# A decode step bound by its loads: 32 small GpSimd loads added beside the K pairs

## The chip, the core and the metric

The kernel runs on one core of a Trainium2 chip. The core has a matrix engine (TensorE, in the profile PE, its weight loads PEld), VectorE (DVE), ScalarE (ACT), GpSimd (POOL) and SyncE (SP), which share one on-chip memory of 128 partitions, and sixteen DMA engines that move data between it and the chip's main memory. SyncE issues the loads; the other engines can issue some too. The metric is the device time of one execution in microseconds (us): the median of the runs.

## The reference

One step of decoding for four sequences mixes two branches with a gate.

```python
x = A_x                                              # [4, 1, 1024]
g = sigmoid((x * gate_w).sum(-1, keepdims=True))
# A: attention of one query per head over a cache, 32 heads of 128, 8192 keys
q = (x @ wq).reshape(4, 1, 32, 128).transpose(0, 2, 1, 3)
p = softmax(einsum("bhqd,bhkd->bhqk", q, k_cache) * 128 ** -0.5)
a = einsum("bhqk,bhkd->bhqd", p, v_cache).transpose(0, 2, 1, 3).reshape(4, 1, 4096) @ wo
# B: with one token per sequence, the token that is selected is always that token
r = x @ w_r
b = x + ((silu(x @ w_gate) * (x @ w_up)) @ w_down) * sigmoid(r)
return g * a + (1 - g) * b
```

All is bfloat16. The two caches are 4 x 32 x 8192 x 128 values each, 268 MB; the weights wq, wo (8.4 MB each) and w_gate, w_up, w_down (7.3 MB each) come on top: some 576 MB are read once, and little is computed with each value.

## The kernel before

Everything large goes through one ring, the tile `ring`: eleven units of 16 KB per partition (2 MB each). A K or V pair is the cache of four heads of one sequence, 8.4 MB in four units, with 64 KB in each partition. There are 32 K pairs and 32 V pairs. A list written out by hand (`plan`) says at which place of the ring each load goes, and `load_pair` (L194) issues it on SyncE, mostly as one DMA (L204), sometimes as two (L209). A load that overwrites a place waits until TensorE has read what was there; SyncE's queue is in order. The order of all work is given by hand (the schedule of TensorE, VectorE and GpSimd is manual): first wq, the three small loads of x, w_r and gate_w into the tile `x` (L228 to L230), and w_gate; then K pairs 0 to 7 (with w_up behind pair 1); then K pair d and V pair d - 8 in turns; then w_down and the last V pairs; at the end wo in pieces of shrinking size.

For a K pair (`k_pair`, L494) there are eight steps. In each, VectorE transposes an eighth of the pair in place (L511, blocks of 32 x 32 words) and TensorE multiplies it, eight matmuls of 512 columns, with the query of the pair laid out in the tile `Z` (L516), summing into `S_ps`. There are two Z tiles, used in turns. GpSimd fills the Z of pair d + 1 with four small copies (`spread`, L492), which stand in its stream at step 4 of pair d. They wait until the matmuls of pair d - 1, the last that read the same Z, have ended. Eight K pairs make a group, behind which softmax runs (VectorE, ScalarE), and GpSimd and ScalarE copy the probabilities into the tile `PB` (L568, L570). V pairs multiply them with V (L587), 64 matmuls each.

The tile `x` (`x6`, L227) has the four rows of x, the row w_r and the row gate_w in partitions 0 to 5, 2 KB in each. TensorE transposes it once at the start (L254), and near the end `add_x` reads its four rows of x again. GpSimd issues no DMA: its stream holds memsets, copies and the waits for them.

Of the kernel before, what the change touches and what calls it, by code (L numbers as in the profile page):

```python
# [8 lines left out]
BF = mybir.dt.bfloat16  # L9
# [103 lines left out]
def kernel(  # L113
# [15 lines left out]
    nc = tc.nc  # L129
    P = 128  # L130
    Bn, Sq, D = A_x.shape
    _, H, Sk, Dh = A_k_cache.shape
    F = B_w_gate.shape[1]
    DT = D // P
# [27 lines left out]
    const = ctx.enter_context(tc.tile_pool(name="const", bufs=1))  # L162
# [31 lines left out]
    def load_pair(src, n, cuts=(1, 1), second=None):  # L194

        place, down = next(plan)
        lo = place * UN
        if second is None:
            second = place * UN + n if place + 4 <= NU else 0
        at = [lo, second]  # L200
        assert second or (n == RING and lo + n == NU * UN and not down)
        halves = [flat[:, x:x + n] for x in at]
        if cuts == (1, 1) and second == lo + n:
            nc.sync.dma_start(out=flat[:, lo:lo + 2 * n], in_=src)  # L204
        else:
            for i, half in enumerate(halves):
                step = n // cuts[i]
                for x in range(0, n, step):
                    nc.sync.dma_start(out=half[:, x:x + step], in_=src[:, i * n + x:i * n + x + step])  # L209
        return halves, list(range(RD))[::-1] if down else list(range(RD))  # L210
# [5 lines left out]
    def bank(ps, z, shape, dtype=F32):  # L216
        b = ps[:, z] if dtype == F32 else ps[:, z].bitcast(dtype)
        n = 1
        for k in shape:
            n *= k  # L220
        names = "abcd"[:len(shape)]
        return b[:, 0:n].rearrange("p (%s) -> p %s" % (" ".join(names), " ".join(names)), **dict(zip(names, shape)))
# [1 line left out]
    N = H * Dh  # L224
    wq_at, _ = load_pair(A_wq.rearrange("(c t) n -> c (t n)", t=DT), DT // 2 * N)
    NX = Bn + 2
    x6 = const.tile([NX, D], BF)  # L227
    nc.sync.dma_start(out=x6[0:Bn], in_=x2)  # L228
    nc.sync.dma_start(out=x6[Bn:Bn + 1], in_=B_w_r.rearrange("(o n) -> o n", o=1))
    nc.sync.dma_start(out=x6[Bn + 1:Bn + 2], in_=gate_w.rearrange("(o n) -> o n", o=1))  # L230
# [8 lines left out]
    n = 1  # L239
# [10 lines left out]
    identb = const.tile([P, P], BF)  # L250
    nc.gpsimd.tensor_copy(out=identb[:], in_=ident[:])
    xw_ps = bank(S0, 2, [DT, NX], BF)
    for t in range(DT):
        nc.tensor.transpose(out=xw_ps[:, t, :], in_=x6[:, t:D:DT], identity=identb[0:NX, 0:NX])  # L254
    xw = const.tile([P, DT, NX], BF)
    nc.vector.tensor_copy(out=xw[:], in_=xw_ps)  # L256
    xT = [xw[:, t, 0:Bn] for t in range(DT)]
# [1 line left out]
    for half in range(2):  # L259
        for e in range(2):  # L260
            nc.gpsimd.tensor_copy(out=R[:, 2 * half + e].rearrange("p (n j) -> p n j", n=4),
                                  in_=ident[:, 64 * half + e:64 * half + 64:2].unsqueeze(1).to_broadcast([P, 4, 32]))
# [205 lines left out]
    def flush():  # L468
        while pending:
            pending.pop(0)()  # L470

    def flush_sums():
        while full:
            full.pop(0)()

    def flush_late():
        while late:
            late.pop(0)()
# [4 lines left out]
    def kv_view(cache, d):  # L483
        b, h0 = heads(d)
        return cache[b, h0:h0 + NQ].rearrange("h (r j) d -> (h r) (j d)", j=2 * JR)

    def spread(d):
        b, h0 = heads(d)
        Z = Zt[d % 2]
        for q in range(NQ):  # L490
            at = slice(QP * q, QP * (q + 1))
            nc.gpsimd.tensor_copy(out=Z[at, :, QP - 1 + QP * q], in_=qa[at, :, h0 + q, b])  # L492

    def k_pair(d):  # L494
        g, t = divmod(d, GD)
        Z = Zt[d % 2]
        if d == 0:
            spread(0)
        if t == 0:
            S_ps[g] = S0  # L500
        sps = S_ps[g]
        ks, order = load_pair(kv_view(A_k_cache, d), RING)
        flush_sums()
        for k, n in enumerate(order):
            unit = ks[n // JT][:, (n % JT) * UN:(n % JT + 1) * UN]
            kn = unit.bitcast(U32).rearrange("p (j h i) -> p h j i", j=CJ, h=2)
            T = unit.rearrange("p (j h i e) -> p h j i e", j=CJ, h=2, e=2)
            s = QP - 1 - (RD * t + n)
            for half in range(2):
                step = 2 * k + half  # L510
                nc.vector.transpose(out=kn[:, half], in_=kn[:, half])  # L511
                if step < 2 and ahead:
                    ahead.pop(0)()
                for e in range(2):
                    for z in range(4):
                        nc.tensor.matmul(sps[:, z, :], lhsT=Z[:, 2 * half + e, s:s + P], rhs=T[:, half, 16 * z:16 * z + 16, :, e],  # L516
                                         start=(t + k + half + e == 0),
                                         stop=(t == GD - 1 and k == RD - 1 and half + e == 2))
                if step == RD and d + 1 < ND:
                    spread(d + 1)  # L520
                if step == RD:
                    flush()
                if step == RD + 2:
                    flush_late()
        if t == GD - 1:
            ahead.extend(softmax(g))
            while g > 0 and ahead:
                ahead.pop(0)()

    def softmax(g):  # L530
        sps = S_ps.pop(g)
        PTs = turned(P, 4 * NB)

        def first():

            nc.vector.tensor_reduce(out=mx[:, 0:1], in_=sps[:].rearrange("p z n -> p (z n)"), axis=AX.X, op=ALU.max)  # L536
            nc.vector.transpose(out=mxT[:].bitcast(U32), in_=mx[:].bitcast(U32))
            gm = stat.tile([P, GD], F32, tag="gm")
            nc.vector.tensor_reduce(out=gm[:], in_=mxT[:].rearrange("p (t r) -> p t r", r=RD), axis=AX.X, op=ALU.max)
            nc.vector.tensor_scalar(out=ng[:].rearrange("p (t r) -> p t r", r=RD), in0=gm[:].unsqueeze(2).to_broadcast([P, GD, RD]),  # L540
                                    scalar1=-scale, scalar2=None, op0=ALU.mult)
            nc.vector.transpose(out=ngT[:].bitcast(U32), in_=ng[:].bitcast(U32))  # L542
            negm = ngT
            rs = stat.tile([P, 1], F32, tag="rs")
            nc.scalar.activation(out=PTs, in_=sps[:].rearrange("p z n -> p (z n)"), func=ACT.Exp, bias=negm[:, 0:1], scale=scale, accum_out=rs[:, 0:1])  # L545
            rs_t[g] = rs

        def second():
            PT = ptp.tile([P, CJ, 32], BF, name="PT", tag="PT")
            nc.vector.transpose(out=PT[:].rearrange("p j i -> p (j i)"), in_=PTs)  # L550
            PT_t[g] = PT
            if g == 0:
                spread_p(0, NW)
            elif g == NG - 1:
                spread_p(GD * g, NW - 1)

        return [first, second]
# [103 lines left out]
    for kind, d in order:  # L661
        if kind == "k":
            k_pair(d)
            if d in side:
                side[d]()
            if d == ND - 1:
                scores.close()
                fin = ctx.enter_context(tc.tile_pool(name="fin", bufs=1, space=PSUM))
                A_ps.extend(fin.tile([P, NB], F32, name=f"acc{n}") for n in range(NH))
                A_ps.append(fin.tile([P, 2, NB], F32, name="led"))  # L670
                wd_piece()
                add_x()
        if (kind, d) == ("v", ND - 1):
            first, second = wo_two(0)
            first()
            last = [second]
        if kind == "v":
            v_pair(d)
        if (kind, d) == ("v", ND - 2):
            o_rows(0, GE)  # L680
# [47 lines left out]
```

## Time and profile before

| What | Value |
|---|---|
| median of 3 runs | 1340.88 us (1340.85 to 1340.89) |
| profiled execution | 1340.96 us, its span 1339.2 us |
| TensorE matmuls, busy | 1031.3 us (77%) |
| VectorE, busy | 638.7 us (48%) |
| GpSimd, busy | 67.0 us (5%) in 174 instructions |
| moved by DMA | 576.14 MB, mean 430 GB/s |
| a K load, issue to landing (median) | 27.5 us |
| packets under 512 bytes | 1436 of 13032 |

The span is the time from the first instruction to the last in the profiled execution; the rest of its time lies around it. A line of waits reads: engine, what it works on and its line, who let it go, then the sum of those waits, how many there were, and the longest. A line of the timeline reads: start and length in us, engine, line, operation, what it writes and reads with shapes, how many instructions are merged, and in brackets the idle time before it and what ended that. In the chain of work that ended last, DMA has 67%, TensorE 22%, VectorE 9%. A queue's line has its packets, its MB and the time of its packets as a share of sixteen engines' span.

### The profile page before, as it was taken

To read this page: it belongs to the slowest core of one execution; us is meant where nothing else is said; L and a number is where in the kernel's file an instruction comes from. 1 tells how busy PE (TensorE), PEld (TensorE's weight loads), DVE (VectorE), ACT (ScalarE), POOL (GpSimd) and SP (SyncE) were. 2 spreads that over 40 slices of the span, in tenths; PEclk is the share of its full clock that TensorE was granted. 3 is DMA by queue.
4 is the path that set the end of the run, shared out by engine and by line. 5 is a ranking of instruction groups with operands and counts; after the bars stand their busy time and mean duration, and the time that the engine had idled before them with its cause. 6 is when DMAs were issued, how large, how long until landed. Compare 5 with 4: busy or idle time off the path is not lost.

```text
span 1339.2 us, 6936 instructions
## 1 busy us (share of the span) xinstructions
PE 1031.3 (77%) x4654; PEld 139.8 (10%) x1486; DVE 638.7 (48%) x385; ACT 57.7 (4%) x58; POOL 67.0 (5%) x174
## 2 busy tenths in 40 slices
PE   2386787887777788777787977777797778687887
PEld 0011000001010010101001110100111011111111
DVE  2285998556553436555352556634345556100001
ACT  0000000100010000100010000100000000110000
POOL 2000000100010000100010000100001000100000
PEclk9697998898888998888889988888998889689999
DMA  9999999999999999999999999999999999999998
GB/s 415 433 437 437 435 437 435 420 438 433 433 435 437 427 433 435 429 438 431 433 431 433 435 439 427 429 433 435 438 430 428 433 429 429 438 429 445 422 422 352
DMA packets 13032, 576.14 MB, mean 430 GB/s; under 512 B 1436, under 2 KB 1700, under 8 KB 1970
## 3 DMA queue, kind: packets, MB, share of 16 engines
q1 hardware_dynamic: 12994, 575.69, 99.6%
q8 instruction: 24, 0.39, 0.1%
q14 instruction: 6, 0.05, 0.0%
q10 hardware_dynamic: 8, 0.00, 0.0%
HBM read 575.68 MB, written 0.01 MB: 430 GB/s over the span
## 4 chain that ended last, share of the span: by engine, by line
DMA 67%; PE 22%; DVE 9%; POOL 0%; ACT 0%; issue 0%; SPq 0%
DMA ring<-in_A_k_cache_dram 53%; PE S_ps L516 15%; DMA ring<-in_A_v_cache_dram 10%; DVE ring L511 9%; PE o_ps L587 5%; DMA ring<-in_B_w_gate_dram 3%; DMA ring<-in_A_wo_dram 2%; PE o_ps L342 1%; POOL PB L570 0%; DVE mx L536 0%; PE led L633 0%; ACT TB L545 0%; PE acc L296 0%; POOL Z L492 0%; PE o_ps L633 0%
## 5 line engine op out<-in xcount | busy, mean ns | idle before, releaser
L511 DVE STREAM_TRANSPOSE ring<-ring 128x2048 uint32<-128x2048 uint32 x256 | 566.5, 2276 | 307.7 <-DMA ring<-in_A_k_cache_dram 307.7
L516 PE MATMUL S_ps<-ring,Z 128*128 128x512 bf16 x2048 | 519.9, 408 | 229.3 <-DVE ring L511 216.1
L587 PE MATMUL o_ps<-ring,PB 128*64 128x512 bf16 x2048 | 457.4, 384 | 35.7 <-DMA ring<-in_A_v_cache_dram 33.3
L516 PEld LDWEIGHTS <-Z 128*128 128x128 bf16 x512 | 53.0, 104 | 683.0 <-issue 683.0
L617 DVE SCALAR_TENSOR_TENSOR OS<-o_ps,mE,OS 128x512 f32<-128x512 f32 x33 | 24.8, 751 | 161.7 <-ACT OS L613 160.2
L587 PEld LDWEIGHTS <-PB 128*64 128x64 bf16 x512 | 56.7, 111 | 428.3 <-issue 427.6
L625 DVE SCALAR_TENSOR_TENSOR OS<-o_ps,mE,OS 128x512 f32<-128x512 f32 x5 | 3.7, 750 | 143.6 <-ACT OS L623 143.6
L492 POOL COPY Z<-qa 32x4 bf16<-32x4 bf16 x128 | 25.8, 201 | 716.7 <-PE S_ps L516 689.6
L570 POOL COPY PB<-PT 32x1024 bf16<-32x1024 bf16 (+3 forms) x23 | 33.4, 1452 | 466.6 <-PE o_ps L587 360.7
L613 ACT ACTIVATE OS<-o_ps,mE 128x512 f32<-128x512 f32 x11 | 7.6, 687 | 671.2 <-PE o_ps L587 671.2
L568 ACT COPY PB<-PT 32x1024 bf16<-32x1024 bf16 (+3 forms) x21 | 30.3, 1444 | 22.4 <-PE o_ps L587 17.4
L545 ACT ACTIVATE TB<-S_ps,mx 128x2048 bf16<-128x2048 f32 x4 | 7.9, 1967 | 321.7 <-DVE mx L542 321.7
L254 PE MATMUL S_ps<-identb,x 6*128 6x6 bf16 x8 | 0.6, 196 | 22.3 <-DMA x<-in_gate_w_dram 22.3
L342 PE MATMUL o_ps<-ring,xw 128*4 128x512 bf16 (+2 forms) x128 | 12.9, 490 | 3.5 <-DMA ring<-in_B_w_gate_dram 3.5
L633 PEld LDWEIGHTS o_ps<-selg,OS 128*128 128x128 f32 x88 | 11.5, 191 | 8.8 <-issue 8.5
L550 DVE STREAM_TRANSPOSE PT<-TB 128x2048 bf16<-128x2048 bf16 x4 | 9.2, 2312 | 6.4 <-ACT TB L545 6.4
L296 PE MATMUL acc<-ring,hT 128*4 128x512 bf16 x54 | 7.9, 466 | 5.5 <-DMA ring<-in_B_w_down_dram 5.5
L536 DVE TENSOR_REDUCE mx<-S_ps 128x1 f32<-128x2048 f32 x4 | 9.1, 2282 | 6.0 <-PE S_ps L516 6.0
L296 PE MATMUL acc<-ring,LT 128*4 128x512 bf16 x64 | 8.8, 378 | 3.3 <-DMA ring<-in_A_wo_dram 2.8
L633 PE MATMUL o_ps<-selg,OS 128*128 128x8 f32 x88 | 10.5, 245 | 0.0
L623 ACT ACTIVATE OS<-o_ps,mE 128x512 f32<-128x512 f32 x5 | 3.4, 687 | 151.2 <-PE o_ps L587 151.2
L256 DVE COPY xw<-S_ps 128x48 bf16<-128x48 bf16 x1 | 0.2, 184 | 17.5 <-PE S_ps L254 17.5
(83 smaller groups left out, 88.4 us busy)
## 6 DMA issues: line engine op xcount, KB each, us to landing
ring<-in_A_v_cache_dram SPq DMA_DIRECT2D x7, 4096.0 KB
ring<-in_A_k_cache_dram SPq DMA_DIRECT2D x6, 4096.0 KB, 33.9
ring<-in_A_v_cache_dram SPq DMA_DIRECT2D x6, 2048.0 KB, 28.9
ring<-in_B_w_gate_dram SPq DMA_DIRECT2D x1, 7168.0 KB
ring<-in_B_w_up_dram SPq DMA_DIRECT2D x1, 7168.0 KB
ring<-in_B_w_down_dram SPq DMA_DIRECT2D x1, 6912.0 KB
ring<-in_A_wo_dram SPq DMA_DIRECT2D x2, 2048.0 KB
ring<-in_A_wo_dram SPq DMA_DIRECT2D x3, 1024.0 KB, 34.5
```

The lines of the kernel that those rows point to most:

```text
L296: nc.tensor.matmul(acc(n), lhsT=lhsT, rhs=rhs, start=start, stop=True, skip_group_check=True)
L342: nc.tensor.matmul(ps[32 * k:32 * k + Bn, z, :].rearrange("p (f r) -> p f r", r=FR)[:, :, lo:hi], lhsT=xT[TW * half + t], rhs=rhs, start=( ...
L492: nc.gpsimd.tensor_copy(out=Z[at, :, QP - 1 + QP * q], in_=qa[at, :, h0 + q, b])
L511: nc.vector.transpose(out=kn[:, half], in_=kn[:, half])
L516: nc.tensor.matmul(sps[:, z, :], lhsT=Z[:, 2 * half + e, s:s + P], rhs=T[:, half, 16 * z:16 * z + 16, :, e], start=(t + k + half + e == 0) ...
L536: nc.vector.tensor_reduce(out=mx[:, 0:1], in_=sps[:].rearrange("p z n -> p (z n)"), axis=AX.X, op=ALU.max)
L550: nc.vector.transpose(out=PT[:].rearrange("p j i -> p (j i)"), in_=PTs)
L568: nc.scalar.copy(out=Bv[at, :, :, q, :], in_=Pv[at])
L570: nc.gpsimd.tensor_copy(out=Bv[at, :, :, q, :], in_=Pv[at])
L587: nc.tensor.matmul(o_ps[w // 2][row:row + NM, w % 2, :], lhsT=PB[:, RD * (d % NW) + n, z].rearrange("p w s j -> p (w s j)"), rhs=vn[:, j0 ...
L617: nc.vector.scalar_tensor_tensor(out=OS[:], in0=o_ps[w // 2][:, w % 2, :], scalar=mE[:, w:w + 1], in1=OS[:], op0=ALU.mult, op1=ALU.add)
L633: nc.tensor.matmul(oT, lhsT=OS[:, q * Dh:(q + 1) * Dh], rhs=selg[:, q].rearrange("p t s -> p (t s)"), start=(q == 0), stop=(q == 3), skip_ ...
```

## The change

The tile of x gets all 128 partitions instead of six, and a function `again` is called in steps 1 and 5 of every K pair. Its first 32 calls, those of K pairs 0 to 15, each issue one DMA from GpSimd's queue: calls 1 to 16 load 31 rows of wq, of 128, 256, ... 2048 bytes, into partitions 32 to 62 of that tile; calls 17 to 32 load a contiguous piece of wq, as 16 rows of 120, 240, ... 1920 bytes, into partitions 64 to 79. Nothing reads what they bring. Later calls do nothing. Since each of the first sixteen overwrites what the one before wrote, it waits on GpSimd for the landing of that one; likewise among the last sixteen. In GpSimd's stream the two loads of a K pair stand ahead of and behind the Z copies of the next.

```diff
-    x6 = const.tile([NX, D], BF)
+    x6 = const.tile([P, D], BF)
+    probe = [0]
+
+    def again():
+
+        j = probe[0]
+        probe[0] += 1
+        if j < 16:
+            c = 64 * (j + 1)
+            nc.gpsimd.dma_start(out=x6[32:63, 0:c], in_=A_wq[0:31, 0:c])
+        elif j < 32:
+            c = 15 * 4 * (j - 15)
+            src = A_wq.rearrange("a b -> (a b)")[0:16 * c].rearrange("(q n) -> q n", q=15)
+            nc.gpsimd.dma_start(out=x6[64:80, 0:c], in_=src)
+
...
-        nc.tensor.transpose(out=xw_ps[:, t, :], in_=x6[:, t:D:DT], identity=identb[0:NX, 0:NX])
+        nc.tensor.transpose(out=xw_ps[:, t, :], in_=x6[0:NX, t:D:DT], identity=identb[0:NX, 0:NX])
...
                 if step == RD + 2:
                     flush_late()
+                if step in (1, 5):
+                    again()
```

The source of calls 17 to 32 is written as 15 rows; in the built program both sides of the DMA have 16 rows of the destination's length.

## The prediction

> **What bounds the kernel now.** I read the page first for its DMA line, because 576 MB in 1339.2 us is the largest thing in it:
>
> ```profile
> DMA  9999999999999999999999999999999999999998
> GB/s 415 433 437 437 435 437 435 420 438 433 433 435 437 427 433 435 429 438 431 433 431 433 435 439 427 429 433 435 438 430 428 433 429 429 438 429 445 422 422 352
> ...
> q1 hardware_dynamic: 12994, 575.69, 99.6%
> q8 instruction: 24, 0.39, 0.1%
> q14 instruction: 6, 0.05, 0.0%
> ```
>
> Every slice but the last is at nine tenths or more, and the SyncE loads (q1) alone fill 99.6% of the sixteen engines' time. Then the busy time by stages, for the K-only stage, the middle and the end (columns: stage, length, the five engines' busy time, granted clock, DMA share, GB/s):
>
> ```profile
> 125.00:165.00 40.00, 31.67 (x135) 3.28 (x34) 36.62 (x18) 0.00 (x0) 1.57 (x8) 1.00 1.02 441
> 700.00:1080.00 380.00, 303.30 (x1313) 38.77 (x360) 186.95 (x102) 12.27 (x10) 15.47 (x44) 0.90 1.00 433
> 1080.00:1340.00 260.00, 206.52 (x987) 33.79 (x406) 57.25 (x51) 16.64 (x23) 10.49 (x11) 0.91 0.98 419
> ```
>
> The DMA share is 1.00 wherever I cut, up to the last 15 us. Third, the waits, for what is late and what has room:
>
> ```profile
> POOL Z L492 <- PE S_ps L516: 689.6, 24, 42.8
> ...
> DVE ring L511 <- DMA ring<-in_A_k_cache_dram: 307.7, 31, 23.6
> ...
> PE S_ps L516 <- POOL Z L492: 5.3, 2, 5.0
> ```
>
> VectorE waits 307.7 us for K; TensorE waits for GpSimd's Z only 5.3 us; GpSimd idles 689.6 us before its Z copies. So the transfers are the bound, and what lengthens the engines' work lengthens the kernel. Last, the room GpSimd has, from the timeline of the K-only stage:
>
> ```profile
> 134.89 0.96 POOL L492 COPY Z<-qa 32x4 bf16<-32x4 bf16 x4 [35.33 <-PE S_ps L516]
> 154.24 0.96 POOL L492 COPY Z<-qa 32x4 bf16<-32x4 bf16 x4 [18.39 <-PE S_ps L516]
> ...
> 156.29 1.89 PE L516 MATMUL S_ps<-ring,Z 128*128 128x512 bf16 x8 [2.11 <-DVE ring L511]
> ```
>
> The Z of K pair 4 is written at 134.89, when pair 2 has ended, and first read at 156.29: 20.4 us of room. K pairs begin 19.35 us apart (154.24 less 134.89).
>
> **The change part by part.** The tile of x grows from 6 to 128 partitions with the same 2 KB in each, and the transposes name its six rows: no instruction differs on TensorE, VectorE, ScalarE or SyncE. Cost 0. All that is new are 32 loads in GpSimd's stream, each waiting for the landing of the one before it (except the first, and the seventeenth, which writes other partitions).
>
> *Bytes.* Loads 1 to 16 bring 31 rows of 128 to 2048 bytes, 31 x 17,408 = 539,648; loads 17 to 32 bring 16 rows of 120 to 1920 bytes, 16 x 16,320 = 261,120. Together 0.80 MB; at the middle stage's 433 GB/s 1.85 us. By packets: the trace keeps each DMA packet with queue, start, length and size, and there 4 bytes take 0.009, 1024 bytes 0.046, 2048 bytes 0.084 and 4096 bytes 0.159 us, so 0.008 us and 0.0375 us per KB. With two of the 31 rows on each engine: 2 x (16 x 0.008 + 17 x 0.0375) = 1.53 us; one of the 16 rows: 16 x 0.008 + 15.9 x 0.0375 = 0.72 us; a 4-byte completion each, 32 x 0.009 = 0.29 us. Sum 2.54 us on each engine. Nothing covers it, as the engines have no idle time.
>
> *Taking turns.* No GpSimd load is in the trace of before. The nearest rows are the instruction fetches, the only packets of another queue amid the loads: 22 of 16 KB on q8 and five of 8 KB on q14. Each stands between two 64 KB packets of one load, and in each case the 64 KB packet behind it is longer. 99% of the 7296 packets of 64 KB take 2.42 to 2.43 us; those behind a q14 packet 0.22 to 0.66 us more (mean 0.51), those behind a q8 packet 0.46 to 0.55 more (mean 0.50). The q14 packets themselves take 0.02 us more than 8 KB on q1 (mean), the q8 packets 0.44 more than 16 KB. So one visit of a foreign queue costs its engine 0.21 to 1.04 us beyond its bytes, 0.54 by the mean of the 8 KB row. I take 0.54, since pieces of at most 2 KB are nearer to 8 KB than to 16. If every engine is visited once for each load (its rows and the completion behind one another), that is 32 x 0.54 = 17.3 us, between 32 x 0.21 = 6.7 and 32 x 1.04 = 33.3.
>
> *GpSimd's time.* Two loads per K pair, issued at perhaps the 0.33 us that SyncE takes for an issue, at most the 3.5 us of GpSimd's longest single instruction (the memset of PB). GpSimd is 5% busy; hidden by the 689.6 us.
>
> *The added wait.* Behind a load that waits stands the next load, and behind that the Z copies of `spread`, for which TensorE waits. From one Z copy to the next go two loads in chain. They may take 19.35 - 0.96 = 18.4 us, so 9.2 us each, and more for a while: the 20.4 us of room over fourteen loads add 1.4 each. A landing from below: issue 0.33 and packets 0.1 us. From above: the 27.5 us that a K load takes from issue to landing. I take about 5.5: issue 0.4, the rest of a 64 KB packet in service (2.4) and one more already begun on the slowest engine (2.4), own packets 0.2. That is under 9.2, so hidden. Were the cover gone, K pair by K pair the excess over 18.4 would go to TensorE, and from there to the SyncE loads, which wait for TensorE to free the ring.
>
> One rule speaks on this. The Trainium skill, "DMA: Bandwidth & Descriptors", section "Anatomy of one DMA", gives a GpSimd load a fixed 2.0 us; in chain that would be estimated at 4 us of the 18.4, hidden as well, and the sum would be the bytes alone.
>
> **Sum.** The profiled execution is 1340.96 us, its span 1339.2 and 1.8 around it; the median of the runs is 1340.88, 0.08 less, and I add to that. 2.54 + 17.3 = 19.8 us: 1360.7, say 1361. With 6.7 and 33.3 in place of 17.3: 1350 to 1377.
>
> **The rivals.**
> *Each packet its own visit.* The fetches show the engine going to the other queue and back within a load, packet by packet. If rows and completion each wait their turn, loads 1 to 16 make three visits on an engine and loads 17 to 32 two: 16 x 3 + 16 x 2 = 80. At 0.54 that is 43.2 + 2.5 = 45.7 us, 1387; at 0.21 and 1.04, 1360 and 1427. The landing would then be near 3 x 2.95 + 0.4 = 9.2 us, just at the bound. For it: those fetches. Against: 64 KB packets say little of how packets of 4 bytes follow one another; the 4-byte completions of q1 take 0.009 us and lengthen nothing.
> *The turn costs nothing.* The longer packet behind a fetch may belong to fetches, not to turns. Then only 1.85 to 2.54 us remain: 1342.7 to 1343.4, within what can be told from no change. Against it: all 27 fetches show it.
> *The 31 rows go through one engine.* 31 is prime; if a load is split only into equal shares, all rows fall on one engine. Each row would wait behind a 64 KB packet: 31 x 2.95 = 91 us while loads are queued, cut to some 30 when TensorE starves and the queue runs dry (27.5 us from issue to landing and the rows). Sixteen of 30 us in chain are 480 us in place of the 8 x 19.35 = 155 us of their K pairs plus 28 of room: up to +297, 1638. At the least one engine carries 31 x 0.54 + 17.3 = 34 us more, 1375. I name 1500, between. The Trainium skill, same page, section "Why a DMA increments its semaphore by 16 and not by 1", has this rule, equal shares over a divisor of the row count, but also names GpSimd loads that are spread in rounded-up shares; no run here shows which.
> *The landing is over the bound with single visits.* At 12 us, eight K pairs lose 2 x 12 + 0.96 - 19.35 = 5.6 us each, 45 less 28 of room, on top of 19.8: 1378.
> *Faster.* In the last 260 us the rate is 419 GB/s against 433, some 8.4 us of transfer time lost at the small wo loads behind the V loads, whose issues wait for landings. Were the later phase of those loads to close such a gap by more than the 2.54 us of added packets, the kernel would gain, at most 8.4 - 2.5 = 5.9: 1335. Against it: by then no new load has run for half the span, and the order of the tail's loads is unchanged.
>
> **How the numbers follow.** One visit 0.40; visit for each packet 0.28; no cost of turns 0.13; one engine 0.11; landing over the bound 0.05; faster 0.03. The time is that of the likeliest, 1361, whose own range is 1350 to 1377. The range starts at 1342, which takes in the bytes alone, and ends at 1427, the far end of 80 visits; it leaves out one engine, most of faster and little else. A change of 0.2%, 2.7 us, is about what a measurement can tell. Bytes alone end within it, nearly all of 0.13, so 0.12 the same; 0.03 faster; 0.85 slower.
>
> **What would show it.** After the change the page should have a further queue with 16 x (16 x 3 + 16 x 2) = 1280 or so packets and 0.80 MB, DMA still at 9 in every slice of the first half, the lost time within about 20 to 560 us where the loads are, and packets of 64 KB at 2.9 to 3.1 us behind the new ones: about 32 x 16 = 512 of them for single visits, near 1280 for the rival. TensorE's wait for Z should stay at some 5 us; if it grows to tens, the landing decides. Slices with less than 9 for DMA there would show TensorE starving the ring, hence one engine. The prediction is wrong below 1350 if turns cost less than the fetches show, above 1377 if they come more often.

## The result and the profile after

The changed kernel takes 1352.3 us (1351.41 to 1353.15 in 3 runs) against 1340.88 before: a ratio of 1.0085, with a 95% interval of 1.0062 to 1.0108. That is 11.4 us slower. The profiled execution is 1352.3 us with a span of 1350.5, so it stands for the runs.

The page of the changed kernel, DMA lines of the forty slices and of the queues:

```profile
DMA  9999999999999999999999999999999999999998
GB/s 417 444 415 433 429 414 412 431 432 422 433 424 418 423 431 433 435 433 435 431 429 431 435 429 431 433 435 434 435 433 433 435 425 434 435 426 441 431 417 340
...
q1 hardware_dynamic: 12994, 575.69, 99.3%
q0 software_dynamic: 1024, 0.80, 0.2%
q8 instruction: 24, 0.39, 0.1%
```

The engines are as busy as before, but q1, with the same 12994 packets and the same bytes, no longer gets all their time, and fewer GB/s are moved in most of the first fifteen slices. A new queue q0 carries the 32 loads in 1024 packets: for each load sixteen with data and sixteen of 4 bytes, the completions. The records do not name engines; two packets for each of sixteen engines fit that number.

The stages, for the K-only stage, the middle and the end (length, busy time of the five engines, granted clock, DMA share, GB/s):

```profile
125.00:165.00 40.00, 31.19 (x134) 3.18 (x33) 35.94 (x18) 0.00 (x0) 2.93 (x11) 1.00 0.99 421
711.00:1091.00 380.00, 305.62 (x1314) 38.84 (x359) 186.52 (x102) 12.27 (x10) 15.36 (x44) 0.90 1.00 433
1091.00:1351.00 260.00, 208.89 (x985) 34.83 (x406) 57.24 (x51) 16.65 (x23) 10.52 (x11) 0.90 0.97 418
```

421 GB/s instead of 441 where the loads are, 433 as before where they are not. The issue of one and the same K load on SyncE, behind the last of the new loads, dates the loss; first before, then after:

```profile
553.58 0.33 SPq L204 DMA_DIRECT2D ring<-in_A_k_cache_dram  x1
```

```profile
564.46 0.33 SPq L204 DMA_DIRECT2D ring<-in_A_k_cache_dram  x1
```

By then 10.9 of the 11.4 us are gone. The waits and GpSimd's timeline show that its new waits do not reach TensorE:

```profile
POOL Z L506 <- PE S_ps L530: 536.7, 23, 40.2
...
DVE ring L525 <- DMA ring<-in_A_k_cache_dram: 319.4, 31, 25.0
...
POOL x L240 <- DMA x<-in_A_wq_dram: 79.8, 10, 9.5
POOL x L236 <- DMA x<-in_A_wq_dram: 69.5, 9, 9.4
...
PE S_ps L530 <- POOL Z L506: 0.3, 1, 0.3
```

```profile
156.31 0.51 POOL L236 DMA_DIRECT2D x<-in_A_wq_dram  x1
165.86 0.51 POOL L236 DMA_DIRECT2D x<-in_A_wq_dram  x1 [9.05 <-DMA x<-in_A_wq_dram]
175.64 0.95 POOL L506 COPY Z<-qa 32x4 bf16<-32x4 bf16 x4 [9.28 <-PE S_ps L530]
```

GpSimd waits 149.3 us for landings, 9.05 us in the case shown, and then still 9.28 us for TensorE before the Z copies. Its time before those copies fell from 689.6 to 536.7 us: the new waits sit inside the old one, and TensorE waits for Z only 0.3 us. VectorE's wait for K grew by 11.7 us, the whole loss.

The packet records say where the engines' time went. Summed over the execution and divided by sixteen engines, q1's packets take 7.4 us longer than before, and the packets of q0 take 2.9 us: 10.3 of the 11.4. In the records nearly every packet starts, within some nanoseconds, where another one ends; such two are taken here as neighbours on one engine. A large packet (32 to 64 KB) behind a data packet of q0 is longer than is usual for its size by 0.19 us in the mean (429 cases), one behind a completion by 0.02 us (437 cases). And the first figure depends on what the packet carries, here for the loads of 16 rows, one row for each engine:

| Row, bytes | 120 | 240 | 480 | 600 | 960 | 1320 | 1920 |
|---|---|---|---|---|---|---|---|
| packet behind it longer by, us | 0.01 | 0.02 | 0.08 | 0.16 | 0.19 | 0.34 | 0.16 |

For the loads of 31 rows it is 0.00 at 512 bytes (two rows of 256 in one packet), 0.13 at 2048 and 0.44 at 4096. So the cost is not simply that of a turn. But each size occurs at one moment of the kernel only, so the rows mix size and moment: two rows of 768 bytes in one packet show 0.00, a row of 720 bytes 0.21. Those of the experiments that use one size throughout separate the two.

### The profile page after: what moved, and what is told of

Its sections match the earlier page's. It is cut to its first block, busy times and chain, and to the rows that moved or that the text cites. A ratio compares the mean times of both kernels' runs of the same rounds, so it can differ in the third digit from the quotient of the medians.

```text
span 1350.5 us, 6973 instructions
## 1 busy us (share of the span) xinstructions
PE 1037.1 (77%) x4654; PEld 141.2 (10%) x1486; DVE 638.6 (47%) x385; ACT 57.8 (4%) x58; POOL 81.8 (6%) x206
## 3 DMA queue, kind: packets, MB, share of 16 engines
q1 hardware_dynamic: 12994, 575.69, 99.3%
q0 software_dynamic: 1024, 0.80, 0.2%
## 4 chain that ended last, share of the span: by engine, by line
DMA 68%; PE 21%; DVE 10%; ACT 0%; issue 0%; SPq 0%; DVEq 0%
DMA ring<-in_A_k_cache_dram 53%; PE S_ps L530 15%; DVE ring L525 10%; DMA ring<-in_A_v_cache_dram 8%; PE o_ps L603 5%; DMA ring<-in_A_wo_dram 5%; DMA ring<-in_B_w_gate_dram 3%; PE o_ps L356 1%; PE acc L310 0%; PE led L649 0%; DVE OS L633 0%; DVE mx L552 0%; ACT TB L561 0%; DVE OS L641 0%; ACT OS L639 0%
## 5 line engine op out<-in xcount | busy, mean ns | idle before, releaser
L633 DVE SCALAR_TENSOR_TENSOR OS<-o_ps,mE,OS 128x512 f32<-128x512 f32 x33 | 24.8, 751 | 162.0 <-ACT OS L629 160.5
L506 POOL COPY Z<-qa 32x4 bf16<-32x4 bf16 x128 | 25.6, 200 | 562.4 <-PE S_ps L530 536.7
L629 ACT ACTIVATE OS<-o_ps,mE 128x512 f32<-128x512 f32 x11 | 7.6, 687 | 674.8 <-PE o_ps L603 674.8
L240 POOL DMA_DIRECT2D x<-in_A_wq_dram x16 | 7.8, 487 | 79.8 <-DMA x<-in_A_wq_dram 79.8
L236 POOL DMA_DIRECT2D x<-in_A_wq_dram x16 | 8.3, 516 | 69.5 <-DMA x<-in_A_wq_dram 69.5
```

The costliest lines, as they stand in the source:

```text
L633: nc.vector.scalar_tensor_tensor(out=OS[:], in0=o_ps[w // 2][:, w % 2, :], scalar=mE[:, w:w + 1], in1=OS[:], op0=ALU.mult, op1=ALU.add)
```

## The experiments

All leave the kernel's own work as it is and change only the 32 loads. "Own" below is the time of the loads' own packets, "longer" that by which the packets of the large loads grew in sum, "idle" time in which an engine had no packet: each for the mean engine, from the packet records of the profiled execution. "Cost" is the median less that of the kernel before in the same comparison.

| Run | Loads | Cost, us | Own | Longer | Idle |
|---|---|---|---|---|---|
| the change | 31 rows to 2 KB, 16 rows to 1.9 KB | 11.4 | 2.9 | 7.4 | 0.1 |
| e1_small | 31 rows of 128 bytes | 1.9 | 1.2 | 0.7 | 0.1 |
| e2_large | 31 rows of 2048 bytes | 21.4 | 6.0 | 15.6 | 0.1 |
| e3_apart | as the change, no near waits | 9.5 | 2.9 | 6.2 | 0.0 |
| e4_four | as the change, four for each K pair | 24.8 | 3.3 | 6.8 | 13.3 |
| e5_pool16 | 16 rows of 2048 bytes | 13.3 | 3.2 | 9.8 | 0.0 |
| e6_sp16 | the same from SyncE | 9.4 | 3.3 | 5.9 | 0.0 |
| e8_one_packet | as e5, marked as one packet | 12.8 | 3.2 | 8.7 | 0.0 |
| e9_512 | 16 rows of 512 bytes | 2.6 | 1.2 | 1.2 | 0.1 |
| e12_rows128 | 128 rows of 256 bytes | 5.5 | 3.7 | 2.1 | 0.0 |
| e13_rows64 | 64 rows of 512 bytes | 10.3 | 3.4 | 6.6 | 0.0 |
| e14_same_source | what e12 reads, into 16 partitions | 15.7 | 3.4 | 11.0 | 0.0 |

In each row, own, longer and idle add up to the cost within 1.4 us; the profiled execution, from which they come, is not always the one at the median. That is the account on which the rest stands.

### First question: turns, sizes or waits

Small rows (e1_small), in place of both kinds of load:

```diff
-        if j < 16:
-            c = 64 * (j + 1)
-            nc.gpsimd.dma_start(out=x6[32:63, 0:c], in_=A_wq[0:31, 0:c])
...
+        if j < 32:
+            nc.gpsimd.dma_start(out=x6[32:63, 0:64], in_=A_wq[0:31, 0:64])
```

> All 32 loads have 31 rows of 128 bytes; places, count and the chain of waits as in the change. Three theories of the 11.4 us that the change costs. (a) Each turn of the other queue costs the engine the same, whatever it carries: 7.4 us of longer 64 KB packets stay, and 32 x (0.018 + 0.009) = 0.9 us of own packets come on top: 1349. (b) The packet behind is longer only where the foreign packet has more than about 500 bytes: nearly nothing stays but the 0.9 us: 1342. (c) The waits of GpSimd for each landing cost the time: landings stay near 9 us, so 1352.

Measured: 1343.05 us, ratio 1.0015 (1.0006 to 1.0024). Its page has 1024 packets in q0 as well, and its waits have one line for the landings:

```profile
q0 software_dynamic: 1024, 0.13, 0.1%
```

```profile
POOL x L235 <- DMA x<-in_A_wq_dram: 144.1, 19, 9.1
```

144 us of waits and 1024 turns cost 1.9 us. Theories (a) and (c) fall; (b), which had 1342, is the one that fits.

Large rows (e2_large) are the same edit with `0:1024` for `0:64`.

> All 32 loads have 31 rows of 2048 bytes, 2.03 MB in all. Own packets 32 x (0.171 + 0.009) = 5.8 us on each engine. (a) equal turns: 5.8 + 7.4 = 13.2, 1354. (b) the cost grows with the packet: 0.44 us behind each 4 KB packet, 14.1 + 5.8 = 19.9, 1361. (c) waits: 1352.

Measured: 1362.51 us, ratio 1.0158 (1.0143 to 1.0173), as (b) has it. The packet behind a 4 KB packet was longer by 0.36 us in the mean, less than the 0.44 taken from the change, but completions added 0.05.

No near waits (e3_apart):

```diff
+        p = 32 + 32 * (j % 3)
...
-            nc.gpsimd.dma_start(out=x6[32:63, 0:c], in_=A_wq[0:31, 0:c])
+            nc.gpsimd.dma_start(out=x6[p:p + 31, 0:c], in_=A_wq[0:31, 0:c])
...
-            nc.gpsimd.dma_start(out=x6[64:80, 0:c], in_=src)
+            nc.gpsimd.dma_start(out=x6[p:p + 16, 0:c], in_=src)
```

> The same 32 loads, written in turn to three separate places, so that each waits for the third before it and not for the one before: the two loads of a K pair are issued at once. (a) and (b): the same packets take the same turns: 1352, with GpSimd's waits for landings near 0. (c) waits: back to 1341 to 1344.

Measured: 1350.67 us, ratio 1.0074 (1.0057 to 1.0091). In the waits of e3_apart the only line that is left for landings is this,

```profile
POOL x L241 <- DMA x<-in_A_wq_dram: 1.3, 1, 1.3
```

and the time stayed within the interval of the change. The waits add nothing that these runs can tell.

Four loads for each K pair (e4_four) probe the bound that the prediction gave for the waits:

```diff
-                if step in (1, 5):
+                if step in (1, 3, 5, 7):
```

> The same 32 loads, but four in each of the first eight K pairs, each waiting for the one before. The bound of the prediction is 18.4 us for the landings between two Z copies. With the 9.0 us measured, four landings and the copies take 37 us of a K pair of 19.4: 17.6 too much in each of eight, 141, less some 28 of room: about 110 to 120 more, 1455 to 1465, with TensorE waiting for Z by that much. If the wait chain does not reach TensorE: 1352. If the landings shorten once TensorE starves the ring: in between, 1390 to 1440.

Measured: 1365.93 us, ratio 1.0185 (1.017 to 1.0201): TensorE now does wait for Z, but far less than expected, and the time is below even the 1390 to 1440 given for landings that shorten. Its waits, its slices and two of its stages:

```profile
PEld L531 <- POOL Z L507: 39.2, 4, 18.2
PE S_ps L531 <- POOL Z L507: 26.0, 2, 17.0
```

```profile
DMA  9999996999999999999999999999999999999998
GB/s 430 432 404 421 413 412 250 434 416 445 429 429 431 431 431 435 433 443 437 429 420 440 433 431 435 431 437 429 431 437 433 431 425 435 440 420 441 431 419 346
```

```profile
200.00:240.00 40.00, 22.96 (x95) 2.37 (x23) 32.55 (x15) 0.00 (x0) 5.35 (x16) 0.79 0.70 292
240.00:280.00 40.00, 29.55 (x127) 3.10 (x31) 22.87 (x14) 5.95 (x4) 8.57 (x19) 0.91 1.00 421
```

The loss sits in one slice, and the timeline of that run shows why it ends there:

```profile
209.47 0.48 POOL L240 DMA_DIRECT2D x<-in_A_wq_dram  x1 [9.06 <-DMA x<-in_A_wq_dram]
219.12 0.48 POOL L240 DMA_DIRECT2D x<-in_A_wq_dram  x1 [9.16 <-DMA x<-in_A_wq_dram]
...
221.29 0.48 POOL L240 DMA_DIRECT2D x<-in_A_wq_dram  x1 [0.69 <-DMA x<-in_A_wq_dram]
223.48 0.48 POOL L240 DMA_DIRECT2D x<-in_A_wq_dram  x1 [1.71 <-DMA x<-in_A_wq_dram]
```

Once TensorE starves the ring (DMA share 0.70 in that stage), the new loads no longer stand behind large ones; the waits fall from 9 to 1 or 2 us and the chain catches up. The engines lost 13.3 us to idleness instead of 110. Besides, the chain starts at 34 us, before the first K pair, which my 28 us of room left out. So the wait does become a bound, as the prediction said, but it limits itself.

### Second question: another queue, or a small packet among large ones

Loads of 16 rows of 2048 bytes, first from GpSimd (e5_pool16), then the same with `nc.sync` (e6_sp16), marked as one packet (e8_one_packet, with `single_packet=True`), and with rows of 512 bytes (e9_512, `0:256`):

```diff
+        if j < 32:
+            p = 32 + 16 * (j % 6)
+            nc.gpsimd.dma_start(out=x6[p:p + 16, 0:1024], in_=A_wq[0:16, 0:1024])
```

> 32 loads of 16 rows of 2048 bytes from GpSimd, in turn to six places, so that none waits for a landing that is near. One row and one completion for each engine and load: own packets 32 x (0.084 + 0.009) = 3.0 us. If the packet behind a foreign one of about 2 KB is some 0.2 us longer, as in the change: 6.4 + 3.0 = 9.4 us, 1350.5. If the cost comes with two rows in one packet: 1344.

> The same 32 loads of 16 rows of 2048 bytes, issued from SyncE, in the queue of the large loads. Own packets 3.0 us. (b1) The longer packet behind belongs to the change of queue: 1344. (b2) It belongs to a small packet between large ones, from whatever queue: 1350.5 as from GpSimd. The loads also take semaphores that SyncE's large loads share; if that delays a large load by more than the 8 us that it is issued ahead, more than either.

Measured: 1354.27 us from GpSimd, ratio 1.0099 (1.0084 to 1.0114), and 1350.33 us from SyncE, ratio 1.007 (1.0055 to 1.0086). GpSimd's is 3.8 us above the 1350.5 expected, with 0.23 us behind data packets and 0.06 behind completions. SyncE's goes through q1, where no queue takes turns, and still has 5.9 of the 9.8 us of longer packets: (b2) holds for most of it. The rest, 3.9 us of 13.3, comes with the other queue. In the records of e6_sp16 the completion follows its data packet at once in nearly all cases; in those of e5_pool16 a large packet stands between them in 485 of 512. So GpSimd's load interrupts the large ones twice, SyncE's once; that this is the whole of the 3.9 us was not shown.

> The loads of 16 rows of 2048 bytes from GpSimd, with row and completion marked as one packet. If that saves the second turn: landings fall from about 9 to about 6 us, and as the completions' turns cost little (0.03 us each) the time stays within 1 us of the version with two packets, 1349.5 to 1350.5. If every turn costs alike: half of the 6.4 us goes, 1347. If the mark changes nothing: 1350.5 and landings of 9 us.

Measured: 1353.74 us, ratio 1.0097 (1.0081 to 1.0114), landings of 10.7 us against 11.7 without the mark, and 1024 packets in q0 again. In the records the completion is still a packet by itself, and the time is the same; whether the engine treats them as one is open.

> 32 loads of 16 rows of 512 bytes from GpSimd, no near waits. Own packets 32 x (0.028 + 0.009) = 1.2 us. If packets up to about 500 bytes lengthen nothing behind them: 1342 to 1343. If the cost goes evenly with the size, a quarter of that of 2048 bytes: 1.6 + 1.2 = 2.8, 1344. If each turn costs alike: 1349.

Measured: 1343.55 us, ratio 1.002 (1.001 to 1.0029). A quarter of the bytes cost 2.6 us, not a quarter of 13.3 but a fifth; the packets of the large loads grew by 1.2 us instead of 9.8. That is half of a quarter of 9.8 (2.5), and the packet behind a data packet is longer by 0.03 us instead of 0.23: the growth is not even, and at 512 bytes it is small but not nothing.

### Third question: what makes the next packet longer

A large load writes all 128 partitions. The new ones write 16 or 31 neighbouring partitions with sixteen packets at about the same time. Two versions spread the same 2048 bytes for each engine over more partitions (e12_rows128 into a tile `land` of 256 bytes in each partition, e13_rows64 into partitions 64 to 127):

```diff
+        if j < 32:
+            nc.gpsimd.dma_start(out=land[:], in_=A_wq[0:P, 0:128])
...
+        if j < 32:
+            lo = 256 * (j % 4)
+            nc.gpsimd.dma_start(out=x6[64:128, lo:lo + 256], in_=A_wq[0:64, 0:256])
```

> 32 loads from GpSimd with 2048 bytes for each engine, as in the version with 16 rows of 2048 bytes, but as 128 rows of 256 bytes, one for each partition, like the rows of the large loads. (d) The packet behind is longer because sixteen engines write at once into sixteen neighbouring partitions, which other engines write too: with every engine on the partitions it has in the large loads, nothing is left but own packets, about 32 x 0.1 = 3.2 us, 1344 to 1345. (e) It is longer because the foreign packet has 2048 bytes: some 0.23 us behind each as before, 1353 to 1354. If the eight rows are eight packets of 256 bytes: own 32 x 0.14 = 4.6 us and, as packets of 256 bytes lengthened nothing, 1346.

> The same bytes as 64 rows of 512 bytes in partitions 64 to 127, four rows for each engine. (d) places: between, near 1348. (e) size of the packet: 1353 to 1354 if the four rows go as one packet, 1344 to 1346 if as four of 512 bytes.

Measured: 1346.68 us, ratio 1.004 (1.0025 to 1.0055), and 1351.54 us, ratio 1.0076 (1.0061 to 1.0091). In all three the records have 512 data packets of 2048 bytes, so (e) would have the same cost in each. The packet behind is longer by 0.23, 0.16 and 0.07 us for 16, 64 and 128 partitions. That is the order that (d) gave, with prices 2 to 4 us above its 1344 to 1345 and 1348: some lengthening stays even with all 128. And the slices of the page of e12_rows128 have nearly the old rate in most of the first half (GB/s):

```profile
GB/s 414 432 435 435 417 435 432 429 427 432 434 435 427 429 432 435 433 437 429 431 433 431 437 435 435 429 431 432 433 431 435 435 425 437 437 422 440 430 418 352
```

What was read differs among the three as well (rows of 2048, 512 and 256 bytes). The last version reads exactly what e12_rows128 reads and writes 16 partitions (e14_same_source):

```diff
+            nc.gpsimd.dma_start(out=x6[p:p + 16, :].rearrange("p (t n) -> p t n", t=8),
+                                in_=A_wq[0:P, 0:128].rearrange("(p t) n -> p t n", t=8))
```

> The same bytes of wq as in the version with 128 rows of 256 bytes (128 pieces of 256 bytes, 8 KB apart), but written into 16 partitions in turn at six places, eight pieces to a partition. (d) If the places that are written make the packet behind longer: as with 16 rows of 2048 bytes, 1353 to 1355. If what is read makes the difference: as with 128 rows, 1346 to 1347.

Measured: 1356.55 us, ratio 1.0116 (1.0099 to 1.0133), with 0.27 us behind each data packet. The source is the same, the packets have the same size and number, and the cost is 15.7 us instead of 5.5. So the place that is written decides most of it, (d). One other thing differs: e12_rows128 writes one place over and over, and GpSimd waits 150.0 us for its landings, while e14_same_source has no such waits. By e3_apart, where taking the waits away did not raise the time, that does not explain 10 us. What in the way to those partitions is contended was not tried.

### The rival of the single engine, on the other queue

The 31 rows from GpSimd went as sixteen data packets for each load, which fits all sixteen engines. From SyncE (e11_sp31, three places in turn):

```diff
+        if j < 32:
+            p = 32 + 32 * (j % 3)
+            nc.sync.dma_start(out=x6[p:p + 31, 0:1024], in_=A_wq[0:31, 0:1024])
```

> 32 loads of 31 rows of 2048 bytes, issued from SyncE, in three places in turn. If a load of 31 rows from SyncE goes through one engine: 31 x 0.084 = 2.6 us of packets for each load on that engine, 83 us in all if it is always the same engine, 1424 or more; if the engine changes from load to load, 83 us spread over sixteen, with the large loads waiting for the one that is behind: 1345 to 1390. If it is spread over sixteen engines as GpSimd's are: 32 x 2 x 0.084 = 5.4 us and the longer packets behind, 1350 to 1358.

Measured: 1456.03 us, ratio 1.085 (1.0832 to 1.0868). The queue line and a stage of this run:

```profile
q1 hardware_dynamic: 14018, 577.72, 94.0%
```

```profile
320.00:420.00 100.00, 70.13 (x291) 8.92 (x80) 38.07 (x21) 0.69 (x1) 1.55 (x8) 0.86 0.82 340
```

The mean engine is idle for 79.5 us more than before, and the packets of q1 take 34.9 us more, 7.5 of them the new packets; together 114.4 of the 117.1 us by which the span of this profiled execution is longer. The new rows' packets take 0.12 us in the mean, and 32 x 31 of them on one engine are 119 us, near the whole cost. In the records the rows of a load follow one another end to start, as on one engine. The rival was a real mechanism, on the queue that the change did not use. That it is always the same engine follows from this account; the records do not name engines. The Trainium skill, "DMA: Bandwidth & Descriptors", section "Why a DMA increments its semaphore by 16 and not by 1", states a rule for it: a load is spread over the largest number of engines, up to sixteen, that divides its row count, which for 31 is one, while some GpSimd loads are spread in rounded-up shares. Both halves agree with these runs: 79.5 us of idle time from SyncE, 0.1 from GpSimd (e2_large).

## Why the prediction was right or wrong

The bound was right. With DMA at its limit, everything the new loads take from the engines came out at the end: 10.3 us in the records, 11.4 in the time. TensorE, VectorE and the tail gave nothing back.

The bytes were about right: 2.54 us predicted, 2.9 measured. Two rows do share a packet, so there was less per-packet time than I counted, but some packets of the fourth and fifth load (1024 and 1280 bytes) took up to 0.3 us longer than others of their size.

The number of turns was wrong, in between the forecast and its first rival. Rows of one engine go as one packet and the completion as another, 64 turns on an engine, not 32 and not 80.

The price of a turn is the term that was mis-sized, and it carried most of the sum: 17.3 us predicted, 7.4 measured. I took 0.54 us from instruction fetches of 8 KB, as the nearest row. A completion's turn costs 0.02 us and a data packet's 0.00 to 0.44, 0.19 in the mean; over the 429 and 437 cases that is 5.6 us on each engine. The other 1.8 us stand on large packets that are not directly behind a new one; why they are longer stays open. Even the low end, 0.21 for each load, would have given 6.7, which is why the time, 1352.3, lies at the lower end of the likeliest case's own range, while the change itself, 11.4 us, is little more than half of the 19.8 forecast. The reason I gave, that taking turns costs time, was the wrong one: e1_small has all the turns and costs 1.9 us, and e6_sp16 has no second queue and costs 9.4. The price hangs on how much is written, and into how few partitions. So the time came out within the range by a mechanism that the prediction did not have, which is partly luck.

"The turn costs nothing", which I gave 0.13, was thus nearer to the mechanism than to the time: it is true of small packets.

GpSimd's added wait was hidden, as predicted, but by less than the prediction's numbers said. The landing took 9.0 us (31 rows) and 9.2 us (16 rows) in the median where I had 5.5; the bound was 9.2, and 10.6 with the room. I counted one turn, behind two packets of 2.42 us; with two turns, each behind one or two such packets, the same working gives an estimate of 5.4 to 10.3 us, and the 9 us lie within it. e4_four shows the bound to be real and its damage to be self-limiting: 13.3 us of idle engines, where I expected 110 before that run. The 28 us of room in two of the rivals come from no row; the row shown gives 20.4, with which the case of landings over the bound would be 1385 and not 1378.

The rule that the prediction weighed from the Trainium skill, "DMA: Bandwidth & Descriptors", section "Anatomy of one DMA", a fixed 2.0 us for a GpSimd load, does not hold here: a load took 9.0 us beside the large loads, and some 2 us (waits of 0.69 and 1.71 behind an issue of 0.48) only where the ring was dry.

The single engine fell for GpSimd, with 1024 packets over sixteen engines, and "faster" fell with the end of the kernel unchanged: 433 GB/s in the middle, 418 against 419 in the last 260 us.

## What to carry to other kernels

In a kernel whose DMA engines are never idle, price a small extra load by engine time: its own packets, plus what it does to the packets behind it, and sum that over the engines. If such a load is needed, spread it over all 128 partitions or keep it to 512 bytes or less for each engine: from GpSimd, 32 loads of the same 32 KB cost 5.5 us one way and 13 to 16 us the other. And a neighbour in the trace that looks like the new operation (here the instruction fetches) gives bounds, not a price, while the operation differs in size and in where it writes.

## What was not expected of the hardware

A 64 KB packet, else 2.42 us with 99% within 0.01, is longer behind a small one by an amount that depends on where the small one wrote: 0.07 us for 2048 bytes per engine spread over 128 partitions, 0.16 over 64, 0.20 to 0.27 over 16. For 512 bytes or less it is 0.00 to 0.08. Packets grow behind small ones of the same queue too (5.9 us in sum from SyncE). And 32 loads of 31 rows of 2048 bytes cost 21.4 us from GpSimd and 114.8 us from SyncE, with the same bytes.
